# Queries and keys turned before the launch, another order of attention parts, and an earlier odd tile, in a fused attention and two-stage MoE kernel

## The chip, the cores and the metric

The kernel runs on one core of a Trainium2 chip. The metric is the device time of one execution in microseconds (us); three runs of the kernel before give the median that it is compared by. The engines are TensorE (PE, and PEld for its weight loads), VectorE (DVE), ScalarE (ACT), GpSimd (POOL), and SyncE (SP), whose queue issues nearly all transfers.

## The reference

```python
# attention: q, k, v are (4, 8, 576, 64), float32
scores = q @ k.transpose(0, 1, 3, 2) / sqrt(64)
kth = np.partition(scores, -32, axis=-1)[..., -32:-31]
scores = np.where(scores >= kth, scores, -1e9)
attn = softmax(scores);  x = (attn @ v) as (2304, 512)
# first MoE: w_a, w_b are (512, 1536), w_out (1536, 512), float64 as drawn
x = (x @ w_a) * (x @ w_b) @ w_out
# second MoE: each token goes to one of 8 experts
logits = normalise(x) @ normalise(expert_emb).T / tau
e = argmax(logits); gate = softmax(logits)[e]
out = gate * (relu(x @ w1[e]) @ w2[e])        # w1 (8, 512, 1024), w2 (8, 1024, 512)
```

Each query attends to its 32 largest scores only. Products are made nearly exact in float32 by splitting operands into a rounded high half and the low rest: three products of halves replace one.

## The kernel before

**Attention.** The work is cut into rows of 128 queries of one head against 576 keys: 144 rows. Queries come in parts, in the order of SEQ: a digit for the batch, and A (queries 0 and 1 of each four), B (2 and 3) and T (the last 64). Each part is done for four pairs of heads in turn, and a pair has two rows per head for A or B and one row for T. One loop over `step` runs the rows as a pipeline: loads ten steps ahead (AHEAD_L), turning from five (AHEAD_P), scores two ahead (AHEAD_Q), top-32 on VectorE at the step itself (`topk`: four `dve.max`, three `dve.match_replace`, then L399), softmax and the turn of the weights two to four steps later, and after a part's last row the product with the values (`mix`). `manual_schedule` fixes the order of PE, DVE, ACT and POOL as it is written out; SP's order is left to the framework.

**Turning queries and keys.** Queries and keys arrive with positions on partitions. `split_qk` makes high and low halves on POOL, `turn_qk` turns them on TensorE (`flip`, L316) into PSUM banks `tr`, and ScalarE (once VectorE) copies the result into `qT` and `kT` (L334 to L352). The first part of a batch and pair ("lead") does the keys, stores them in `kT_d`, and later parts load them from there. A score is two products: (key high, key low) with (query high, low) and with (query low, high).

**First MoE.** Tokens are done in nine groups of 256 (GROUPS), as soon as all queries of a group are there. `moe1` yields after every few matmuls (L729, L676), and `background` runs it between the attention's pieces, by a budget per step:

```python
rates.append((WORK * sum(x < w for x in opens) - spent[0]) / (w - step))
return max(min(rates, default=STEP), 0.0) + SHARE
...
share[0] = max((STEP0 if step < S0 else min(level(step), STEP)) - cost, 0.0) / max(n, 1)
```

`opens` are the steps at which groups count as open, nine after their last row (`opens.append(i + TL + 3 + RD)`), `cost` is what the step's attention costs by the planner's own figures, and `n` the number of places at which the budget is spent. The weights' halves lie in `wab_d` and are loaded again for each group. Each 128 tokens that are done are routed (`route`, L779 on): norm, logits against the expert vectors (L791), the largest, the rank within the expert, and a row written to `row_d` and its index to `ids_d`.

**Second MoE.** After the last attention row the weights of the first expert come in units of 1 MB (`unit`: load `raw`, split into `u` by ACT and DVE, L1109 and L1110), paced by the last groups of the first MoE. Tokens of the first 16 of 18 routed chunks give the first expert two full tiles (`first_expert`), which run while the last tokens are routed. Then comes its odd tile of 80 rows (`last_tile`), and then the other seven experts, each in two stages with transposed hidden values (L1179, L1353), with the next expert's rows gathered and turned (`turn_x`) in between. Only TensorE's order is written out by hand here.

## Time and profile before

| what | us |
|---|---|
| median of 3 runs (lowest to highest) | 1232.67 (1230.98 to 1233.19) |
| profiled execution, its own time | 1234.76 |
| its span, first to last instruction | 1233.0 |
| busy in the span: PE | 1133.8 (92%) |
| PEld | 982.4 (80%) |
| DVE | 916.2 (74%) |
| ACT | 822.8 (67%) |
| POOL | 728.8 (59%) |

Shares are means over stages that differ: VectorE is nearly always busy while the attention runs and little used after it. Matmul bars overlap, as matmuls are pipelined, so a step on TensorE is better priced from one start to the next than by its bar. The granted clock of TensorE is 0.97 of full over the span.

### The profile page before, as it was taken

How to read it: one execution, taken by the hardware profiler on the slowest of the kernel's cores; microseconds unless marked ns; L12 is line 12 of the kernel's file. 1: busy time of each engine (PE TensorE's matmuls, PEld its weight loads, DVE VectorE, ACT ScalarE, POOL GpSimd, SP SyncE). 2: the span in 40 equal slices, each digit the busy share in tenths (PEclk: the TensorE clock that was granted, in tenths of full speed). 3: DMA queues.
4: the chain of work that ended last, by engine and by line, in shares of the span. 5: the costliest groups of instructions: out<-in, count | busy, mean ns of one | idle time of the engine just before them, and what ended most of it. 6: DMA issues, size and time to landing. Idle time of an engine off the chain costs nothing. (4 is left out here: it accounts for less than half of the span.)

```text
span 1233.0 us, 23911 instructions
## 1 busy us (share of the span) xinstructions
PE 1133.8 (92%) x8124; PEld 982.4 (80%) x8125; DVE 916.2 (74%) x2015; ACT 822.8 (67%) x1970; POOL 728.8 (59%) x1195
## 2 busy tenths in 40 slices
PE   5767798999999998999999999999989989999996
PEld 4445566787897887898888888888878869999995
DVE  8998999999999998999999999940210225655540
ACT  5777888987878886787878877754442435554441
POOL 5565687877776876776778677665545420322211
PEclk9788899999999999999999999999999999999998
DMA  7334647676784667667666667757977245665530
GB/s 237 117 123 135 209 165 258 211 255 214 234 261 148 183 218 222 204 190 225 190 183 200 200 202 208 219 181 227 339 259 220 88 129 205 204 218 194 179 103 28
DMA packets 129200, 240.05 MB, mean 195 GB/s; under 512 B 24896, under 2 KB 74176, under 8 KB 129074
## 3 DMA queue, kind: packets, MB, share of 16 engines
q1 hardware_dynamic: 125170, 228.74, 58.6%
q0 software_dynamic: 3904, 9.75, 2.1%
q8 instruction: 65, 1.06, 0.4%
q14 instruction: 61, 0.50, 0.2%
HBM read 198.38 MB, written 40.31 MB: 194 GB/s over the span
## 5 line engine op out<-in xcount | busy, mean ns | idle before, releaser
L394 DVE MAX8 t<-y 128x8 f32<-128x576 f32 x432 | 311.7, 749 | 2.7
L409 POOL TENSOR_TENSOR z<-s,z 128x576 f32<-128x576 f32 x144 | 206.8, 1436 | 88.7 <-ACT z L406 84.1
L729 PE MATMUL ab<-xg,wab 128*128 128x256 f32 x1398 | 212.3, 290 | 3.6 <-DMA wab<-wab_d 2.0
L397 DVE MATCH_REPLACE8 y<-t,y 128x576 f32<-128x576 f32 x288 | 214.0, 743 | 0.0
L729 PEld LDWEIGHTS ab<-xg,wab 128*128 128x128 f32 x1398 | 184.2, 191 | 7.5 <-issue 2.0
L729 PE MATMUL ab<-raw,wab 128*128 128x256 f32 x1152 | 173.1, 288 | 4.0 <-ACT gab L743 3.0
L428 PE MATMUL tr<-ident,z 128*128 128x128 f32 x720 | 133.8, 285 | 45.6 <-ACT z L411 41.4
L729 PEld LDWEIGHTS ab<-raw,wab 128*128 128x128 f32 x1152 | 150.6, 189 | 6.8 <-ACT gab L743 3.6
L431 ACT ACTIVATE wt<-tr 128x384 f32<-128x384 f32 (+2 forms) x320 | 128.2, 412 | 39.9 <-PE tr L428 38.7
L374 ACT ACTIVATE s<-tr 128x288 f32<-128x288 f32 x288 | 118.0, 410 | 51.9 <-PE tr L373 41.1
L428 PEld LDWEIGHTS tr<-ident,z 128*128 128x128 f32 x720 | 88.8, 144 | 65.1 <-ACT z L411 53.8
L676 PE MATMUL x<-wo,gh 128*128 128x512 f32 x432 | 137.1, 399 | 0.0
L1163 POOL DMA_INDIRECT out_dram<-o,ids x24 | 31.4, 1307 | 170.7 <-ACT o L1162 116.5
L373 PE MATMUL tr<-kT,qT 128*128 128x288 f32 x512 | 125.5, 331 | 5.5 <-ACT s L374 4.2
L1110 DVE TENSOR_TENSOR u<-raw,u 128x1024 fp32r<-128x1024 f32 x64 | 76.2, 1222 | 60.8 <-ACT u L1109 60.8
L411 ACT ACTIVATE z<-z,bi 128x576 f32<-128x576 f32 x144 | 112.2, 779 | 0.3 <-POOL z L409 0.3
L406 ACT ACTIVATE z<-s,bi 128x576 f32<-128x576 f32 x144 | 111.3, 773 | 0.0
L663 POOL TENSOR_TENSOR gab<-gab 128x256 f32<-128x256 f32 x108 | 81.8, 757 | 49.1 <-ACT gab L743 31.2
L394 DVE MAX8 t<-s 128x8 f32<-128x576 f32 x144 | 107.1, 743 | 4.5 <-ACT s L374 4.5
L397 DVE MATCH_REPLACE8 y<-t,s 128x576 f32<-128x576 f32 x144 | 106.9, 743 | 0.0
L663 POOL TENSOR_TENSOR gl<-gab,gh 128x256 fp32r<-128x256 f32 x108 | 80.6, 747 | 44.4 <-ACT gh L663 39.8
L373 PEld LDWEIGHTS tr<-kT,qT 128*128 128x128 f32 x512 | 88.8, 205 | 15.2 <-ACT s L374 4.6
(201 smaller groups left out, 2243.5 us busy)
## 6 DMA issues: line engine op xcount, KB each, us to landing
wab<-wab_d SPq DMA_DIRECT2D x192, 512.0 KB, 4.6
raw<-in_moe_w_dram SPq DMA_DIRECT2D x28, 1024.0 KB, 5.5
wab_d<-wab SPq DMA_DIRECT2D x24, 512.0 KB, 3.9
kT<-kT_d SPq DMA_DIRECT2D x20, 576.0 KB, 5.2
vs<-in_v_dram SPq DMA_DIRECT2D x36, 256.0 KB, 3.1
kT_d<-kT SPq DMA_DIRECT2D x16, 576.0 KB, 4.6
raw<-in_moe_w_a_dram SPq DMA_DIRECT2D x12, 512.0 KB, 4.1
raw<-in_moe_w_b_dram SPq DMA_DIRECT2D x12, 512.0 KB, 4.5
```

The lines of the kernel that those rows point to most:

```text
L373: pe.matmul(p, l, r, start=(i == 0), stop=(i == len(terms) - 1))
L374: act.activation(t.s[:, cs], p, AF.Copy, scale=SCALE)
L394: dve.max(v, cur)
L397: dve.match_replace(out=rest, in_to_replace=v, in_values=cur, imm_value=LOWEST)
L406: act.activation(t.w, t.s, AF.Relu, bias=t.bi[:, 1:2], scale=-HUGE)
L409: pool.tensor_tensor(t.w, t.s, t.w, op=OP.subtract)
L411: act.activation(t.w, t.w, AF.Exp, bias=t.bi[:, 0:1], accum_out=t.o.sm[:, t.slot : t.slot + 1])
L428: pe.transpose(pt[:, i * P : (i + 1) * P], t.w[:, k0 : k0 + P], ident)
L431: act.activation(th[:, sl, w], pv[:, :, src], AF.Copy)
L663: pend.pop(0)[1]()
L676: pe.matmul(px[t], g[:, ts], wo[:, w, f], start=(f == 0 and i == 0), stop=(f == NF - 1 and i == 2))
L729: pe.matmul(ps_[i], wt[:, a, c, :], xg[x][:, c, :], start=(j == 0 and f not in begun), stop=(j == len(terms) - 1),)
```

## The change

Queries and keys are laid out by numpy before the launch, with the 64 elements of a head on the first axis and positions on the second, in the order in which the rows take them. The kernel loads each into both halves of the partitions. ScalarE rounds the high half and GpSimd subtracts the low one (VectorE for the very first part), and the turns on TensorE, their PSUM banks and evictions go. `split_qk` yields after each pair of operations, and is drawn twice a step without spending the background's budget. The two products of a score are now with the query's high half twice and with its low half twice.

The order of parts is another (SEQ): the third batch's T stands by itself, behind the fourth batch's A and T and ahead of the third's B. SHARE is smaller, and the term for turning leaves the cost. In the first MoE one forced drain of pending steps and one yield in routing are added, and yields are left out once the first expert's weights are in. A paced unit of weights is split two chunk loads later than it was. The odd tile of the first expert is gathered and turned inside `first_expert`, its hidden halves are turned between matmuls of its own two stages, and the gates that hold back the splits of later weights name both halves of a unit. The diff, cut to its core ("..." where lines are left out):

```diff
-SEQ = "0A 0B 1A 0T 1BT 2A 2BT 3AT 3B"
+SEQ = "0A 0BT 1A 1BT 2A 3AT 2T 2B 3B"
...
-SHARE = 2.1
+SHARE = 1.75
...
-FX = (0, 5)
+FX = (3, 5)
...
-    B, H, S, D = q.shape
+    B, H, D, S = q.shape
...
-    identr = cst.tile([P, P], F32R, name="identr")
-    dve.tensor_copy(identr, ident)
...
+        def both(src, dst):
+            for g in range(2):
+                sp.dma_start(dst[g * D : (g + 1) * D], src.rearrange("h d j -> d h j"))
+
         def load_q(o):
-            r = wk.tile([P, 5, D], F32, name="qr")
-            h0 = 2 * o.pr
-            for h in range(2):
-                if o.M:
-                    sp.dma_start(
-                        r[:, 2 * h : 2 * h + 2, :].rearrange("p c d -> p (c d)"),
-                        q[o.b, h0 + h, 0:512, :].rearrange("(p c) d -> p c d", c=4)[:, o.c : o.c + 2, :].rearrange(
-                            "p c d -> p (c d)"
-                        ),
-                    )
-                if o.tail:
-                    sp.dma_start(r[h * 64 : (h + 1) * 64, 4, :], q[o.b, h0 + h, 512:576, :])
+            r = wk.tile([P, 2, 320], F32, name="qr")
+            hs = slice(2 * o.pr, 2 * o.pr + 2)
+            if o.M:
+                both(q[o.b, hs, :, o.c * P : o.c * P + o.M], r[:, :, : o.M])
+            if o.tail:
+                both(q[o.b, hs, :, 512:576], r[:, :, o.M : o.N])
             return r
 
         def load_k(o, b, pr):
-            h0 = 2 * pr
-            kr = wk.tile([P, 9, D], F32, name="kr", bufs=1)
-            sp.dma_start(
-                kr[:, 0:8, :].rearrange("p (h c) d -> p h (c d)", h=2),
-                k[b, h0 : h0 + 2, 0:512, :].rearrange("h (p c) d -> p h (c d)", c=4),
-            )
-            for h in range(2):
-                sp.dma_start(kr[h * 64 : (h + 1) * 64, 8, :], k[b, h0 + h, 512:576, :])
-            o.kr = kr
-
-        def split_k(o):
-            kr = o.kr
-            ks = wk.tile([P, 9, 2, D], F32R, name="ks", bufs=1)
-            if o.n:
-                yield from split(ks[:, :, 0, :], ks[:, :, 1, :], kr)
-            else:
-                act.activation(ks[:, :, 0, :], kr, AF.Copy)
-                dve.tensor_tensor(ks[:, :, 1, :], kr, ks[:, :, 0, :].bitcast(F32), op=OP.subtract)
-            o.ks = ks
+            o.kr = wk.tile([P, 2, S], F32, name="kr", bufs=1)
+            both(k[b, 2 * pr : 2 * pr + 2], o.kr)
...
         def split_qk(o):
+
+            eng = pool if o.n else dve
             o.qT = wk.tile([P, 2, 512], F32R, name="qT")
             o.kT = wk.tile([P, 2, S], F32R, name="kT", bufs=2)
             o.wt = [None, None]
             o.sm = wk.tile([P, 8], F32, name="sm", bufs=3)
             o.rc = wk.tile([P, 8], F32, name="rc", bufs=3)
+            todo = []
+            if o.lead:
+                for h in range(2):
+                    todo.append((o.kT[:, h], o.kT[D:, h], o.kr[:, h], o.kr[D:, h], h))
+            else:
+                sp.dma_start(o.kT.bitcast(F32).rearrange("p h j -> p (h j)"), kT_d[o.b * NP + o.pr])
+            if o.M:
+                hi, lo = (o.qT[:, a].rearrange("p (h j) -> p h j", h=2) for a in range(2))
+                todo.append((hi, lo, o.qr[:, :, : o.M], o.qr[:, :, : o.M], 0))
             if o.tail:
                 o.qm = qms.pop(0)
                 qms.append(o.qm)
                 for h in range(2):
+                    hi, lo = (o.qm[:, a, h, h * 64 : (h + 1) * 64] for a in range(2))
+                    r = o.qr[:, h, o.M : o.N]
+                    todo.append((hi, lo, r, r, 0))
+            due = None
+            for hi, lo, r, x, last in todo + [(None,) * 5]:
+                if due:
+                    lo_, x_, hi_, last_ = due
+                    eng.tensor_tensor(lo_, x_, hi_.bitcast(F32), op=OP.subtract)
+                    if last_:
+                        sp.dma_start(kT_d[o.b * NP + o.pr], o.kT.bitcast(F32).rearrange("p h j -> p (h j)"))
+                if r is None:
+                    return
+                act.activation(hi, r, AF.Copy)
+                due = lo, x, (lo if lo.shape[0] != hi.shape[0] else hi), last
+                yield
 
...
-            if o.lead:
-                yield from split_k(o)
-            qs = wk.tile([P, 5, 3, D], F32R, name="qs", bufs=1)
-            js = slice(0 if o.M else 4, 5 if o.tail else 4)
-            yield from split(qs[:, js, 0, :], qs[:, js, 1, :], qr[:, js])
-            pool.tensor_scalar(qs[:, js, 2, :], qr[:, js], 1.0, 1.0, op0=OP.mult, op1=OP.mult)
-            o.qs = qs
...
-            def flip(pt, c, x):
-                pe.transpose(pt[:, c * P : (c + 1) * P], x.rearrange("p a d -> p (a d)"), identr)
...
-            for a in range(2 if o.M else 0):
-                pt = ps.tile([P, 512], F32R, name="tr", bufs=NTR)
-                for c in range(4):
-                    flip(pt, c, qs[:, c, a : a + 2, :])
-                if a or o.n:
-                    act.activation(o.qT[:, a, :], pt.bitcast(F32), AF.Copy)
-                else:
-                    dve.tensor_copy(o.qT[:, a, :], pt.bitcast(F32))
-                yield 0.22
...
+                while pend and pend[0][0] <= f - 2:
+                    tick()
...
+            if now[0] >= NRW and not ended:
+                yield 0.0
...
             act.activation(lg, pl[:, :NE], AF.Copy)
-            yield 0.0
+            if not ended:
+                yield 0.0
...
             if flips and (flips[0].n < 2 or parts[flips[0].n - 2].left == 0):
-                while flips[0].qs is None:
-                    piece()
-                if not run(flips[0].flip):
-                    flips.pop(0)
+                with tc.high_priority(offset=FG):
+                    if next(flips[0].flip, flips) is flips:
+                        flips.pop(0)
...
-            if flips:
-                cost, n = cost + 0.44, n + 2
...
+                if slot_ == 2:
+                    flip_next()
             if 0 <= step + AHEAD_Q < NRW:
                 live[step + AHEAD_Q].o.left -= 1
-            for _ in range(2):
-                flip_next()
...
+                    if i and c == 2:
+                        split_unit(i - 1)
             else:
                 sp.dma_start(raw, src)
+                split_unit(i)
+
+        def split_unit(i):
+            raw = raws.pop(i)
             u = w2p.tile([P, 2, 4, 512], F32R, name="u", bufs=UB)
             if gate[0] is not None:
-                act.activation(u[:, 0, 0, 0:1], gate[0], AF.Copy)
+                act.activation(u[:, 0, 0:4:2, 0:1], gate[0], AF.Copy)
...
+        def split(pt, x, xT, m):
+            for c in range(KC):
+                pe.transpose(pt[:, c * P : c * P + m], x[:m, c * P : (c + 1) * P], ident[:m, :m])
+            pv = pt.rearrange("p (c j) -> p c j", c=KC)[:, :, :m]
+            hi, lo = xT
+            act.activation(hi, pv, AF.Copy)
+            dve.tensor_tensor(lo, pv, hi.bitcast(F32), op=OP.subtract)
...
+                    if (t, f) == (1, 5):
+                        reached.append(f)
...
+        split_unit(UB - 1)
+        ended.append(True)
...
+        spare = wx.tile([P, 2, KC, m0], F32R, name="yT", bufs=1)
+        x0 = wx.tile([P, RW], F32, name="xg", bufs=2 * NT3)
+        x0T = [spare[:, i] for i in range(2)]
+        pick(x0, ids[0][:m0, NT3 - 1, 0:1])
+        while not reached:
+            next(early0)
+        split(bank("tr"), x0, x0T, m0)
+        for _ in early0:
+            pass
...
-            t, m = NT3 - 1, m0
-            xs = [None] * t + [wx.tile([P, RW], F32, name="xg", bufs=2 * NT3)]
-            xT = [wk.tile([P, KC, cap], F32R, name=f"xT{i}")[:, :, : caps[0]] for i in range(2)]
-            hT = [wk.tile([P, NF2, cap], F32R, name=f"hT{i}", bufs=1)[:, :, :m] for i in range(2)]
-            pick(xs[t], ids[0][:m, t, 0:1])
+            hT = [wk.tile([P, NF2, cap], F32R, name=f"hT{i}", bufs=1)[:, :, :m0] for i in range(2)]
             nx = gather(NE - 1)
-            turn_x((xs, xT), t)
-            hs = []
+            hs = [result(), x0[:, :DM]]
+
+            def turn_h(half):
+                split(bank("tr"), hs[half], [y[:, half * 4 : half * 4 + 4] for y in hT], m0)
+
             for half in range(2):
                 u = units[half]
                 p = bank("h")
                 n = 0
                 for a, b in TERMS:
                     for c in range(KC):
-                        pe.matmul(p[:m], xT[b][:, c, t * P :], u[:, a, c, :], start=(n == 0), stop=(n == 11))
+                        pe.matmul(p[:m0], x0T[b][:, c, :], u[:, a, c, :], start=(n == 0), stop=(n == 11))
                         n += 1
-                hs.append(result())
-                act.activation(hs[-1][:m], p[:m], AF.Relu)
+                        if half and n == 7:
+                            turn_h(0)
+                act.activation(hs[half][:m0], p[:m0], AF.Relu)
             turn_x(nx, 0, NE - 1)
-            for half, h in enumerate(hs):
-                pt = bank("tr")
-                for j in range(4):
-                    pe.transpose(pt[:, j * P : j * P + m], h[:m, j * P : (j + 1) * P], ident[:m, :m])
-                pv = pt.rearrange("p (j k) -> p j k", j=4)[:, :, :m]
-                hi, lo = (y[:, half * 4 : half * 4 + 4] for y in hT)
-                act.activation(hi, pv, AF.Copy)
-                dve.tensor_tensor(lo, pv, hi.bitcast(F32), op=OP.subtract)
-            gate[0] = hT[0][:, 4, 0:1]
-            upto(2 + UB)
             p = bank("y")
             for f in range(NF2):
                 stage2(0, f, p, hT[0][:, f], hT[1][:, f])
+                if f == 1:
+                    turn_h(1)
                 if f in FX:
                     turn_x(nx, 1 + FX.index(f), NE - 1)
-            put(p, xs[t], ids[0][:m, t, 1:2], m, result())
+                if f == FX[0]:
+                    gate[0] = hT[0][:, 4:6, 0:1]
+                    upto(2 + UB)
+            put(p, x0, ids[0][:m0, NT3 - 1, 1:2], m0, result())
             return nx
...
-                if f % 4 == 0:
+                if f == 0 or (f == 4 and e > 1):
...
-                            gate[0] = hT[0][:, NF2 - 1, 0:1] if f == 0 else None
+                            gate[0] = hT[0][:, NF2 - 2 :, 0:1] if f == 0 else None
...
+def turned(a):
+
+    import numpy as _np
+
+    b, h, _, d = a.shape
+    rows = a[:, :, :512].reshape(b, h, 128, 4, d).transpose(0, 1, 4, 3, 2).reshape(b, h, d, 512)
```

## Rows read from the trace of the kernel before

**Rows 1.** Windows, all engines: length, busy us and instructions per engine, TensorE clock, DMA.
```profile
250.00:455.00 205.00, 200.13 (x1607) 173.97 (x1606) 203.38 (x475) 167.93 (x448) 157.44 (x281) 1.00 0.68 212
...
669.00:778.00 109.00, 105.13 (x794) 88.98 (x793) 102.51 (x237) 86.22 (x221) 78.03 (x144) 0.98 0.67 200
778.00:826.00 48.00, 46.44 (x357) 42.07 (x357) 35.43 (x88) 31.40 (x79) 32.17 (x62) 1.00 0.66 205
```
**Rows 2.** The same windows, line L399 alone, which runs once for each row.
```profile
250.00:455.00 205.00, 5.40 (x40) 1.00 0.68 212
455.00:669.00 214.00, 5.43 (x40) 0.99 0.68 208
669.00:778.00 109.00, 2.71 (x20) 0.98 0.67 200
778.00:826.00 48.00, 1.10 (x8) 1.00 0.66 205
```
**Rows 3.** Line L316 (PE: ns min/median/max), then its windows: PE, PEld.
```profile
L316 PE MATMUL tr<-identr,qs x288: 219/247/369, 6.7 to 770.7; 128*128 128x128 f32 x144
...
L316 PE MATMUL tr<-identr,ks x144: 220/248/367, 5.5 to 686.1; 128*128 128x128 f32 x144
...
455.00:669.00 214.00, 14.29 (x118) 12.73 (x118) 0.99 0.68 208
669.00:778.00 109.00, 6.03 (x51) 5.36 (x51) 0.98 0.67 200
```
**Rows 4.** Timeline of PE around four turns: start us, length us, what.
```profile
405.94 0.46 PE L316 MATMUL tr<-identr,ks 128*128 128x128 f32 x4
406.23 0.70 PE L729 MATMUL ab<-xg,wab 128*128 128x256 f32 x4
```
**Rows 5.** Timeline of the start.
```profile
3.95 0.68 ACT L264 ACTIVATE ks<-kr 128x576 fp32r<-128x576 f32 x1 [1.69 <-DMA kr<-in_k_dram]
4.66 0.76 DVE L265 TENSOR_TENSOR ks<-kr,ks 128x576 fp32r<-128x576 f32 x1 [0.86 <-ACT ks L264]
...
8.29 2.37 PE L373 MATMUL tr<-kT,qT 128*128 128x288 f32 x8 [0.37 <-DVE qT L352]
```
**Rows 6.** Groups by form: count, busy us, mean ns, idle before.
```profile
L350 ACT ACTIVATE qT<-tr 128x512 fp32r<-128x512 f32 x63 | 37.4, 608 | 2.7 <-PE tr L316 2.5
...
L229 POOL TENSOR_TENSOR ks<-kr,ks 128x576 fp32r<-128x576 f32 x15 | 21.5, 1434 | 0.4
```
**Rows 7.** Timeline of PE, the sixth group's beginning, its end, and the seventh's beginning.
```profile
675.22 0.63 PE L729 MATMUL ab<-raw,wab 128*128 128x256 f32 x4
...
765.97 0.55 PE L428 MATMUL tr<-ident,z 128*128 128x128 f32 x3 [0.70 <-ACT z L411]
...
770.41 0.53 PE L316 MATMUL tr<-identr,qs 128*128 128x128 f32 x4 [1.02 <-POOL qs L302]
771.88 0.90 PE L428 MATMUL tr<-ident,z 128*128 128x128 f32 x3 [0.94 <-ACT z L411]
...
777.52 0.75 PE L729 MATMUL ab<-xg,wab 128*128 128x256 f32 x4
```
**Rows 8.** Timeline of PE near the first MoE's end.
```profile
894.27 1.68 PE L729 MATMUL ab<-raw,wab 128*128 128x256 f32 x12
...
921.19 1.15 PE L791 MATMUL ab<-enT,x1T 128*128 128x8 f32 x8 [3.03 <-ACT x1T L787]
922.19 2.91 PE L729 MATMUL ab<-xg,wab 128*128 128x256 f32 x12
```
**Rows 9.** Timeline of PE, the first expert's odd tile and the second expert.
```profile
1000.82 5.74 PE L1297 MATMUL h<-u,xT 128*80 128x512 f32 x24 [1.02 <-ACT xT L1158]
...
1010.44 0.53 PE L1305 MATMUL tr<-ident,o 80*128 80x80 f32 x4 [3.16 <-DVE xT L1159]
1010.84 1.57 PE L1191 MATMUL y<-u,hT 128*80 128x512 f32 x3
...
1034.78 1.36 PE L1353 MATMUL y<-hT,u 128*128 128x264 f32 x9 [1.49 <-DVE hT L1184]
```

More of the change, by code (lines that the diff above doesn't have):

```diff
@@ L345, in turn_qk @@
-            for a in range(2 if o.M else 0):
-                pt = ps.tile([P, 512], F32R, name="tr", bufs=NTR)
-                for c in range(4):
-                    flip(pt, c, qs[:, c, a : a + 2, :])
-                if a or o.n:
-                    act.activation(o.qT[:, a, :], pt.bitcast(F32), AF.Copy)
-                else:
-                    dve.tensor_copy(o.qT[:, a, :], pt.bitcast(F32))
-                yield 0.22
+                    hi, lo = (o.qm[:, a, h, h * 64 : (h + 1) * 64] for a in range(2))
@@ L806, in route @@
             dve.tensor_scalar(st[:, 2:3], m8[:, 0:1], st[:, 1:2], -1.0, op0=OP.mult, op1=OP.mult)
-            yield 0.0
+            if not ended:
+                yield 0.0
             ex = mk.tile([P, NE], F32, name="ex")
@@ L1004, in fused_kernel @@
                 en_turn(mp, e_sb)
-            for o in coming[:1]:
-                if step >= o.first - AHEAD_P or (step >= o.first - AHEAD_P - 2 and not flips):
-                    pieces.append(split_qk(o))
-                    coming.pop(0)
-                    while step < EAGER and pieces:
-                        piece()
+            while step < EAGER and pieces:
+                piece()
             while 0 <= step + AHEAD_Q < NRW and live[step + AHEAD_Q].o in flips:
@@ L1091, in unit @@
             e = slice(0, 1) if n == 0 else bass.ds(expert[NE - n], 1)
-            raw = w2p.tile([P, 4, 512], F32, name="raw", bufs=2)
+            raws[i] = raw = w2p.tile([P, 4, 512], F32, name="raw", bufs=2)
             if part < 2:
@@ L1111, in unit @@
             units[i] = u
-        units = {}
+        units, raws = {}, {}
         expert = [0] * NE
@@ L1152, in turn_x @@
             m = rows_of(r)[t]
-            pt = bank("tr")
-            for c in range(KC):
-                pe.transpose(pt[:, c * P : c * P + m], xs[t][:m, c * P : (c + 1) * P], ident[:m, :m])
-            pv = pt.rearrange("p (c j) -> p c j", c=KC)[:, :, :m]
-            hi, lo = (y[:, :, t * P : t * P + m] for y in xT)
-            act.activation(hi, pv, AF.Copy)
-            dve.tensor_tensor(lo, pv, hi.bitcast(F32), op=OP.subtract)
+            split(bank("tr"), xs[t], [y[:, :, t * P : t * P + m] for y in xT], m)
         def put(p, xg, ids, m, o):
@@ L1240, in fused_kernel @@
                 next(early0, None)
-        for _ in early0:
-            pass
-        mo.close()
-        if "xh" in dbg:
-            sp.dma_start(dbg["xh"][:, :, : batches * S], xh_d[:, :, : batches * S])
-            sp.dma_start(dbg["xl"][:, :, : batches * S], xl_d[:, :, : batches * S])
-        if "row" in dbg:
-            nr = sum(GROUPS[done - 1])
-            sp.dma_start(dbg["row"][:nr], row_d[1 : nr + 1])
-            sp.dma_start(dbg["ids"], ids_d)
-        if batches < 4:
-            return
-        wk = ph.enter_context(tc.tile_pool(name="wk2", bufs=2))
         m0 = rows_of(0)[-1]
@@ L1271, in fused_kernel @@
             )
+        spare = wx.tile([P, 2, KC, m0], F32R, name="yT", bufs=1)
[7 more added lines that the diff above has]
+            pass
+        mo.close()
+        if "xh" in dbg:
+            sp.dma_start(dbg["xh"][:, :, : batches * S], xh_d[:, :, : batches * S])
+            sp.dma_start(dbg["xl"][:, :, : batches * S], xl_d[:, :, : batches * S])
+        if "row" in dbg:
+            nr = sum(GROUPS[done - 1])
+            sp.dma_start(dbg["row"][:nr], row_d[1 : nr + 1])
+            sp.dma_start(dbg["ids"], ids_d)
+        if batches < 4:
+            return
+        wk = ph.enter_context(tc.tile_pool(name="wk2", bufs=2))
         banks.append(ph.enter_context(tc.tile_pool(name="ps3", bufs=1, space=PSUM)))
```

38 lines of the change are left out of this document (6 added, 32 removed).

## The prediction

> **What bounds the kernel now.** I read the windows first, all engines, over the attention from its row 36 on. (A "row" is one pass of the loop: 128 queries of one head, four MAX8 and three MATCH_REPLACE8 on VectorE.) From 250 to 455 us VectorE is busy 203.4 of 205 us and TensorE 200.1: both are full [rows 1]. To know which sets the pace I counted rows by L399, which runs once a row: 40 rows in 205 us, 5.125 us each, with VectorE idle 1.6 us in all, so VectorE sets it there; then 40 in 214 us, 20 in 109, and 8 in 48, which is 6.0 us a row [rows 2]. In that last stretch VectorE is busy only 35.4 of 48 us while TensorE has 46.4 [rows 1]: there TensorE sets the pace. The four counts and 36 rows before them are all 144, so after about 826 us no row is left, and TensorE carries the rest alone. There are two regimes, then, and TensorE work that is taken out is worth something only where TensorE is last, or where the freed time is filled with MoE work that is otherwise done after the attention. After that I read TensorE's timeline at the seam between two token groups, at the longest wait of the first MoE's end, and in the last part; they stand with the steps that they price.
>
> **The change, part by part.**
>
> *The turns go.* The code has 9 turns for each of 16 first parts, 8 for each of 32 parts with 256 queries and 2 for each of 16 tails: 144 + 256 + 32 = 432, and the trace has 288 + 144 [rows 3]. Four of them end 0.29 us after they begin (405.94 to 406.23), though their bars last 0.46 [rows 4], so one costs 0.0725 us and all 31 us. 51 of them lie in 669 to 778 us, 118 in 455 to 669 [rows 3], and the others before, where VectorE sets the pace or TensorE has idle time anyway.
>
> *What replaces them.* ScalarE loses the evictions (63 of the queries' are 37.4 us; half as many of the keys' and small ones come on top) and gets one 128x576 copy per head of keys (32 at L264's 0.68 us, 21.8 us [rows 5]), one 128x512 copy per part (32 at L350's 0.608 us, 19.5 us) and 32 small copies: about even [rows 6]. GpSimd loses the rounding passes and the 15 key subtractions over 128x576, 21.5 us, and gets 30 subtractions of as many columns on 64 partitions; at the same 1.434 us that is 43 us [rows 6], 21.5 more, against the passes that go. I take this at nothing, because GpSimd is idle 47.6 of 205 us from 250 to 455 [rows 1]; what it costs if a subtraction comes late is the second rival. The loads of queries and keys move twice the bytes (a copy each for the upper and the lower partitions), in 16 fewer issues (two per key load where three were). They are issued ten rows ahead, some 51 us at 5.125 us a row, and the reload of keys from kT_d stays at 20 issues; SP's queue has nothing new to wait for. Nothing again.
>
> *The start.* The first score matmul runs at 8.29 us. Now three copies on ScalarE and three subtractions on VectorE come before it, where copy, subtraction, turn and eviction were. Copies of 0.68 us from the landing at 3.95, and subtractions of 0.76 behind the first of them (L264, L265 [rows 5]), end at about 7.0, so that the score matmul can go at 7.1. I take 1.2 us; bounds 0 and 1.5.
>
> *Rows 36 to 116.* 250 to 455 us has nothing to give: VectorE is full. In the next 40 rows, 214 us against 40 x 5.125 = 205, there are 9 us that VectorE loses to late scores and sums. 118 turns fall here, 8.6 us of TensorE. I take 5 of the 9; bounds 0 and 9, since part of it may come from the seams between groups, which stay.
>
> *The new order and SHARE.* The planner counts a group as open nine rows after its last query row. By the old order that is at rows 24, 40, 56, 80, 96, 116, 136, 136, 152; by the new one at 24, 44, 60, 80, 96, 116, 120, 136, 152. Its rate is the smallest of (46.3 x groups open before w, less what is spent) / (w - row), plus SHARE, at most STEP = 5.4. Old: from row 24 on 46.3 x 6 / 112 = 2.48 a row up to row 136, and there 2 x 46.3 for 12 rows, over the cap. New: about 2.5 up to row 116, and there (370.4 - 231.5) / 36 = 3.9, plus 1.75 = 5.6: the cap holds from row 116 on. The attention's own cost in the planner's units is 0.54 + 0.48 + about 0.7, 1.7 a row, so 3.7 a row goes to the MoE for 32 rows, where it was 2.5 for the first 20 of them. A row at the cap takes 6.0 us [rows 2], so the attention ends later: rows 116 to 144 take 28 x 6.0 = 168 us instead of 157. That costs nothing in itself, because TensorE is then full all the way and the work it does comes off the end. From row 116 to the end of the first MoE I therefore count TensorE alone. The 51 turns go (51 x 0.0725 = 3.7 us). The sixth group (675 to 767 us) no longer waits for its successor, which is open at row 120: the idle 0.70, 1.02 and 0.94 us there go, with some 1.5 us of a half clock behind them (three transposes took 0.90 us, where they had taken 0.55), 4.2 us [rows 7]. Together 7.9; bounds 0 and 7.9.
>
> *The end of the first MoE.* Group routing now yields once more before its logits, and ScalarE no longer stands at the raw weights' landing, as a unit is split two chunks later. The 3.03 us that TensorE waits for x1T at 921 us, and the 12 matmuls behind it that take 2.91 us where 1.68 is usual [rows 8], make 4.4 us with a few slow matmuls more. I take all; bounds 0 and 4.4.
>
> *The last part.* TensorE waits 1.02 us for the odd tile's xT, 3.16 for DVE xT, and 1.49 for DVE hT [rows 9]. The tile is now fetched and turned inside the expert before, the second ReLU writes to a buffer of its own, and the weights' splits are gated behind both halves. With a half clock after the 3.16 (three matmuls take 1.57 us) that is 6.7 us; I take 6.0, as the fetch may come late at its new place; bounds 2 and 6.7.
>
> **Sum.** 1234.76 - 1.2 - 5 - 7.9 - 4.4 - 6.0 = 1210.3 us for the profiled execution, whose span is 1233.0. The median of the runs is 1232.67, 2.1 lower, so I forecast 1208. With all bounds at their ends it is 1203 to 1231.
>
> **A rule against this sum.** By TensorE's weight-load time, 174.0 of 205 us from 250 to 455, a seventh of it would be free where its matmul bars show it full [rows 1]. The Trainium skill (Perfetto Trace Analysis, section Identifying the Most-Contended Engine) says that the bars are the poorer measure of headroom and the weight loads the better one. What it would make of the time is the third rival, at 1184 instead of 1208.
>
> **The rivals.**
>
> *The freed time is not filled.* VectorE sets the pace up to row 116, and the planner's pace is fixed when the program is written, so that it can't react. If groups become ready later than it counts (stores and reloads of xh and xl), rows 116 to 136 run as before, and what is left is the start, the wait for x1T and the last part: 1232.7 - 11.6 = 1221. For it: those 20 rows take 109 us as it is, with both engines near full [rows 1, 2]. Against: the seams at 675 and 777.5 us come within two rows of the planner's 116 (669 us) and 136 (778 us) [rows 2, 7].
>
> *Slower.* The low halves are now the last step before the scores, on GpSimd, whose queue also holds the mask subtraction that waits for ScalarE. If one subtraction of 1.434 us [rows 6] stands in the way of each of the 32 full parts, VectorE loses 32 x 1.43 = 46 us: 1254. It decides from 24.5 / 32 = 0.77 us a part. For it: GpSimd is three quarters busy [rows 1]. Against: lists of at most six pieces are drawn two to a row from five rows ahead, and scores start two rows ahead.
>
> *TensorE has room in the attention.* If 15% of its time, 0.77 us a row, can still be filled, the 32 rows at the cap take that much more work without growing: 32 x 0.77 = 24.6 us, 1184. Against it: at the cap a row takes 6.0 us while VectorE is idle a quarter of it [rows 1, 2].
>
> **How the numbers follow.** Forecast 0.69 (own range 1199 to 1219); not filled 0.14; slower 0.09; room 0.05; no change at all, since gains and losses cancel, 0.03. Less than 0.2% (2.5 us) can't be told from no change here. Faster 0.69 + 0.14 + 0.05 = 0.88, same 0.03, slower 0.09. The range 1193 to 1228 leaves out the slower case, the case of room, no change, and some 3 in 100 of the rest.
>
> **What would show it.** No L316; score matmuls that wait for GpSimd no more than the turns did; rows 36 to 76 still at about 5.1 us; the rows after row 116 at about 6 us, with TensorE without idle; no pause between the sixth and the seventh group; the last row later than 826 us, and the last part beginning some 18 us earlier; no wait over 1 us in its first 20 us. The prediction is wrong if rows before 116 take over 5.3 us, if score matmuls wait for GpSimd, or if weights (wab) come late in the stretch at the cap.

## The result, and the profile after

The changed kernel takes 1223.87 us in the median of four runs (1214.99 to 1226.78), the kernel before 1232.93 us beside it: a ratio of 0.9898, 95% interval 0.9868 to 0.9927 (the two medians alone divide to 0.9927; the ratio is what is compared below). The forecast was 1208 us, range 1193 to 1228: the sign and the range hold, the medians' gain of 9.1 us is less than half of the 24.5 that were summed. The profiled execution took 1223.5 us, its span 1221.6 us.

I cut both spans at the same marks: the first pass of the row marker (L399 before, L354 now), its rows 36 and 116, and the eviction that begins the last block's routing, with which the first MoE ends. In us:

| stretch | before | after | difference | forecast |
|---|---|---|---|---|
| start to row 0 | 18.3 | 21.4 | +3.1 | -1.2 |
| rows 0 to 36 | 232.1 | 223.9 | -8.2 | 0 |
| rows 36 to 116 | 418.9 | 431.6 | +12.7 | -5 |
| row 116 to the end of the first MoE | 306.1 | 291.4 | -14.7 | -12.3 (7.9 and 4.4) |
| last part | 257.6 | 253.3 | -4.3 | -6.0 |
| sum | 1233.0 | 1221.6 | -11.4 | -24.5 |

**The attention.** The windows of the changed kernel, all engines: length, then busy us and instructions of PE, PEld, DVE, ACT and POOL, TensorE's clock, DMA share and GB/s.
```profile
245.30:676.90 431.60, 401.95 (x2987) 341.46 (x2987) 409.29 (x951) 336.37 (x870) 333.60 (x541) 0.98 0.75 226
676.90:829.20 152.30, 150.66 (x1157) 134.17 (x1158) 124.29 (x296) 109.15 (x273) 107.69 (x196) 1.00 0.74 232
...
309.40:391.10 81.70, 77.99 (x587) 67.71 (x586) 81.32 (x187) 64.99 (x169) 60.92 (x105) 1.00 0.76 218
391.10:610.70 219.60, 204.89 (x1514) 174.66 (x1514) 204.86 (x479) 171.50 (x440) 175.04 (x275) 0.98 0.72 217
```
The first line is rows 36 to 116. VectorE has 409.3 us of work for 80 rows, 5.116 each, which is its floor; 22.3 us are idle. The third line is rows 48 to 64, and they stand at the floor (5.11 us a row). The fourth is rows 64 to 104, which take 5.49; before, these rows stood so:
```profile
393.50:606.20 212.70, 205.84 (x1584) 177.89 (x1583) 204.66 (x479) 168.89 (x439) 161.04 (x271) 0.99 0.66 201
```
The second, rows 116 to 140, is the stretch at the cap: TensorE is idle 1.6 of 152.3 us, and a row takes 6.35.

What VectorE and TensorE wait for in rows 36 to 116 (total us, times, longest), a view for each engine:
```profile
DVE rc L394 <- POOL rc L392: 15.2, 12, 2.4
DVE st L760 <- POOL st L754: 3.6, 1, 3.6
DVE t L349 <- ACT s L329: 1.6, 1, 1.6
...
PE tr L383 <- ACT z L366: 22.0, 24, 4.1
```
Before, the first stood at 6.1 us in 5 waits and the last at 6.3 us in 6. The timeline shows one of the waits for the sum, in row 46, GpSimd and then VectorE:
```profile
295.93 0.74 POOL L619 TENSOR_TENSOR gl<-gab,gh 128x256 fp32r<-128x256 f32 x1 [2.24 <-ACT lg L757]
297.42 0.74 POOL L619 TENSOR_TENSOR gab<-gab 128x256 f32<-128x256 f32 x1 [0.76 <-ACT gab L701]
...
298.32 1.44 POOL L364 TENSOR_TENSOR z<-s,z 128x576 f32<-128x576 f32 x1
299.83 0.24 POOL L392 TENSOR_SCALAR rc<-sm 128x4 f32<-128x4 f32 x1
...
297.48 0.19 DVE L767 TENSOR_SCALAR st<-m,st 128x1 f32<-128x1 f32 x1
300.11 0.18 DVE L394 RECIPROCAL rc<-rc 128x4 f32<-128x4 f32 x1 [2.43 <-POOL rc L392]
```
The sums are complete at 298.1, when the exponential has ended; the addition of 1e-9 stands behind the next row's mask subtraction on GpSimd, and VectorE, in order, behind the addition. No low half stands in GpSimd's queue here: it had itself stood 2.24 and 0.76 us for ScalarE. The longest wait, VectorE's 3.6 us for the router's `st`, is in row 73, which took 8.7 us; GpSimd, and then TensorE:
```profile
430.50 1.12 POOL L799 DMA_INDIRECT ids_d<-tk,ds  x1 [0.29 <-POOL ds L798]
...
436.15 1.42 POOL L301 TENSOR_TENSOR kT<-kr,kT 64x576 fp32r<-64x576 f32 x1 [3.33 <-DMA ids_d<-tk,ds]
...
441.99 0.90 PE L383 MATMUL tr<-ident,z 128*128 128x128 f32 x3 [4.12 <-ACT z L366]
```
GpSimd stood still for 3.33 us ahead of a key subtraction until the routing's index write, issued at 430.50, had landed; behind it in the queue stood a mask subtraction, a low half of queries and then `st`. TensorE, which had stood 4.12 us, was at its lower clock, 1.2 GHz (granted 0.50), from 439.4 to 446.2 us, and its three transposes took 0.90 us where 0.55 is usual.

GpSimd's new work, line L301: its form for keys (ns min/median/max), then its windows in the two stretches (VectorE, GpSimd).
```profile
L301 POOL TENSOR_TENSOR kT<-kr,kT x30: 1401/1424/1488, 17.2 to 579.4; 64x576 fp32r<-64x576 f32 x30
```
```profile
309.40:391.10 81.70, 0.00 (x0) 5.86 (x9) 1.00 0.76 218
391.10:610.70 219.60, 0.00 (x0) 36.39 (x34) 0.98 0.72 217
```
The low halves take GpSimd 5.9 us in the rows at the floor and 36.4 us in the slow stretch, whose 34 instructions hold 16 key subtractions of 1.42 us; before, GpSimd had 161.0 us of work in these rows, now 175.0. A subtraction over 64 partitions costs what one over 128 did [rows 6].

**The start.** ScalarE, VectorE and TensorE, each by its timeline:
```profile
6.16 1.25 ACT L306 ACTIVATE kT<-kr 128x576 fp32r<-128x576 f32 x2 [3.90 <-DMA kr<-in_k_dram]
...
16.34 0.68 ACT L306 ACTIVATE kT<-kr 128x576 fp32r<-128x576 f32 x1 [5.24 <-DMA kr<-in_k_dram]
...
17.97 0.76 DVE L349 MAX8 t<-s 128x8 f32<-128x576 f32 x1 [2.28 <-ACT s L329]
...
9.08 3.49 PE L328 MATMUL tr<-kT,qT 128*128 128x288 f32 x13 [0.49 <-DVE qT L301]
```
The first copy runs at 6.16 us where it ran at 3.95 [rows 5]: the keys, twice the bytes, land 2.2 us later (6.1 us in the median from issue to landing in the first 27 us, before 3.9). The second pair's keys land at 16.3 us, with VectorE waiting behind.

**The seam, the end of the first MoE, the last part**, in TensorE's timeline:
```profile
749.71 0.62 PE L632 MATMUL x<-wo,gh 128*128 128x512 f32 x2
750.17 0.64 PE L685 MATMUL ab<-xg,wab 128*128 128x256 f32 x4
...
915.48 2.16 PE L685 MATMUL ab<-xg,wab 128*128 128x256 f32 x16
917.52 1.06 PE L751 MATMUL ab<-enT,x1T 128*128 128x8 f32 x8
918.43 0.72 PE L685 MATMUL ab<-xg,wab 128*128 128x256 f32 x4
...
992.60 4.54 PE L1270 MATMUL h<-u,yT 128*80 128x512 f32 x19
996.98 0.44 PE L1112 MATMUL tr<-ident,o 80*128 80x80 f32 x4
997.21 1.35 PE L1270 MATMUL h<-u,yT 128*80 128x512 f32 x5
...
1007.04 0.50 PE L1141 MATMUL h<-xT,u 128*128 128x264 f32 x2 [0.56 <-DVE u L1070]
...
1017.84 3.19 PE L1141 MATMUL h<-xT,u 128*128 128x264 f32 x24 [0.88 <-DVE hT L1146]
```
The seventh group follows the sixth without a pause, at 750 where it was 777.5 us [rows 7]. The router's matmuls no longer wait for x1T, and nothing runs slow behind them [rows 8]. The waits of 1.02, 3.16 and 1.49 us of [rows 9] are gone; small ones, the two longest shown, take their place.

### The profile page after: what moved, and what is told of

Same layout as the page of the kernel before. It is cut to its first block, busy times and chain, and to the rows that moved or that the text cites. A ratio compares the mean times of both kernels' runs of the same rounds, so it can differ in the third digit from the quotient of the medians.

```text
span 1221.6 us, 22925 instructions
## 1 busy us (share of the span) xinstructions
PE 1098.5 (90%) x7692; PEld 940.3 (77%) x7693; DVE 916.3 (75%) x2014; ACT 810.7 (66%) x1923; POOL 732.0 (60%) x1150
## 3 DMA queue, kind: packets, MB, share of 16 engines
q8 instruction: 62, 1.02, 0.3%
## 5 line engine op out<-in xcount | busy, mean ns | idle before, releaser
L685 PE MATMUL ab<-xg,wab 128*128 128x256 f32 x1398 | 207.3, 289 | 1.8 <-DMA wab<-wab_d 1.8
L685 PEld LDWEIGHTS ab<-xg,wab 128*128 128x128 f32 x1398 | 183.3, 191 | 4.8 <-DMA wab<-wab_d 2.4
L685 PE MATMUL ab<-raw,wab 128*128 128x256 f32 x1152 | 170.4, 290 | 3.6 <-ACT gab L701 3.5
L685 PEld LDWEIGHTS ab<-raw,wab 128*128 128x128 f32 x1152 | 150.7, 192 | 6.9 <-ACT gab L701 4.5
```

Of the source, the lines that this page charges most:

```text
L685: pe.matmul(ps_[i], wt[:, a, c, :], xg[x][:, c, :], start=(j == 0 and f not in begun), stop=(j == len(terms) - 1),)
```

## The experiments

Each was timed beside the kernel before on its own chip. The stretches (us) are those of the table above, from the profiled executions, which differ from the medians by up to some 8 us (those of e2 and e3 were the slowest of their runs).

| run | ratio, 95% interval | row 0 | 0-36 | 36-116 | to end of first MoE | last |
|---|---|---|---|---|---|---|
| changed kernel | 0.9898 (0.9868-0.9927) | 21.4 | 223.9 | 431.6 | 291.4 | 253.3 |
| e1 key low halves on VectorE | 1.0006 (0.9988-1.0024) | 27.1 | 227.7 | 434.6 | 286.3 | 254.0 |
| e2 old order | 1.0095 (1.0060-1.0131) | 21.4 | 231.4 | 438.9 | 310.5 | 253.0 |
| e3 three key tiles | 0.9868 (0.9838-0.9899) | 24.8 | 225.6 | 430.5 | 291.2 | 255.2 |
| e4 before + last part | 0.9914 (0.9883-0.9944) | 18.7 | 231.4 | 419.7 | 302.8 | 253.6 |
| e5 sums on VectorE | 0.9865 (0.9830-0.9900) | 21.2 | 225.7 | 425.6 | 285.8 | 252.1 |
| e6 e5 with SHARE 2.1 | 1.0043 (1.0018-1.0068) | 21.3 | 231.6 | 439.2 | 290.6 | 252.0 |
| e7 e5 with the old order | 1.0136 (1.0102-1.0170) | 21.3 | 233.5 | 432.2 | 304.2 | 252.2 |
| e8 e4 with sums on VectorE | 0.9946 (0.9926-0.9967) | 18.4 | 230.7 | 419.7 | 300.2 | 252.3 |
| e9 no negation | 0.9810 (0.9780-0.9840) | 21.7 | 220.6 | 428.8 | 289.9 | 252.4 |
| e10 no addition | 0.9885 (0.9845-0.9924) | 21.3 | 224.6 | 428.6 | 290.4 | 256.1 |
| e11 three key tiles, e9, e10 | 0.9846 (0.9803-0.9888) | 26.2 | 225.1 | 422.1 | 288.7 | 252.5 |
| e12 e4 with e9, e10 | 0.9897 (0.9867-0.9927) | 18.2 | 230.4 | 418.2 | 298.7 | 252.2 |

**e1, the keys' low halves on VectorE.**
```
-    eng.tensor_tensor(lo_, x_, hi_.bitcast(F32), op=OP.subtract)
+    (dve if lo_.shape[0] < P else eng).tensor_tensor(lo_, x_, hi_.bitcast(F32), op=OP.subtract)
```


> The changed kernel with its 28 later key subtractions on VectorE in place of GpSimd (the first two are on VectorE already); nothing is left out. Theory 1, GpSimd is the engine that is late in rows 36 to 116: 20 of the 28 lie there or just before, 1.42 us each, so GpSimd loses about 28 us of work there and VectorE gains under 20 us against some 75 us of idle time in that stretch; the VectorE waits on the sum of GpSimd (15.2 us in 12 waits in 250 to 676) go back to about the 6 us of before, and rows 36 to 116 from 431.6 to 419 to 423 us; median 1212 to 1217, ratio to before 0.983 to 0.987. Theory 2, the order of the parts makes the stretch long: rows 36 to 116 stay within 3 us of 431.6 and the ratio within 0.988 to 0.993. Theory 3, VectorE was short: rows 36 to 116 get longer by the added VectorE work, up to 15 us, ratio up to 1.0.

Rows 36 to 116, VectorE's only waits, and the window:
```profile
DVE kT L301 <- ACT kT L306: 1.0, 2, 0.5
```
```profile
254.70:689.40 434.70, 403.32 (x3024) 342.69 (x3022) 431.09 (x971) 338.21 (x874) 311.30 (x528) 0.99 0.74 224
```
The waits of 20.4 us fall to 1.0: without the key subtractions on GpSimd VectorE doesn't wait for it at all. But VectorE is the engine that sets the pace there, and has 431.1 us of work in 434.7. Theory 3 holds for the time, theory 1 for the waits. (At the start VectorE now stands 10.9 us for copies of keys, and row 0 comes 5.7 us later.) It doesn't show that the stretch would fall to 410 us if the subtractions cost nothing, since a slower VectorE also gives the others more time in each row.

**e2, the old order.**
```
-SEQ = "0A 0BT 1A 1BT 2A 3AT 2T 2B 3B"
+SEQ = "0A 0B 1A 0T 1BT 2A 2BT 3AT 3B"
```


> The changed kernel with the parts in the order of before; the rest as in the changed kernel. Theory 2, the order (two batches' leads next to each other, the first group opened four rows later) costs rows 36 to 116: they go from 431.6 to at most 421 us, row times above 5.8 us vanish, and the median falls by 8 to 12 us, ratio about 0.980 to 0.984, unless the end of the attention gives some of it back because its tail by itself stands late again. Theory 1, GpSimd late whatever the order: the same sum of row times, its late rows only spread over other places; ratio 0.988 to 0.994. Opposite: the new order is what shortened rows 0 to 36 or row 116 to the end of the first expert layer, and the old one gives that back: ratio 0.995 or more.

The opposite case came: slower than the changed kernel by 2%, and worse in each stretch from row 0 to the end of the first MoE (+7.5, +7.3, +19.1 us). In rows 36 to 116, VectorE's and TensorE's longest waits:
```profile
DVE rc L394 <- POOL rc L392: 16.8, 10, 3.1
DVE t L349 <- ACT s L329: 7.8, 8, 3.5
...
PE tr L383 <- ACT z L366: 37.8, 27, 6.2
```
Theory 2 falls: the new order doesn't cost rows 36 to 116, it helps them. GpSimd's lateness is there in either order; in the old one rows 56 to 64 take 46.2 us, where 40.7 is the floor, with no key subtraction in them. The new order by itself, with turns on TensorE, wasn't tried.

**e3, three key tiles of one head.**
```
-    o.kr = wk.tile([P, 2, S], F32, name="kr", bufs=1)
-    both(k[b, 2 * pr : 2 * pr + 2], o.kr)
+    o.kr = []
+    for h in range(2):
+        o.kr.append(wk.tile([P, 1, S], F32, name="kr", bufs=3))
+        both(k[b, 2 * pr + h : 2 * pr + h + 1], o.kr[h])
...
```


> The changed kernel with the key tile cut into one for each head and three of them in place of the one tile for both heads, so that the next pair's first head is loaded while the pair before is still being split; four loads for each pair in place of two. If late key data cost time: the row marker 0 comes 2 to 3 us earlier (21.4 to about 18.5), the 3.3 us stand of GpSimd before the key subtraction at 432.8 goes, its 5.9 us of such waits between 250 and 676 fall below 2, and the median falls by 3 to 8 us, ratio 0.983 to 0.988. If they were covered behind the first rows' other work and GpSimd's slack: ratio within 0.003 of 0.990 and only the start moves.

The first score matmul and VectorE's first weight unpacking:
```profile
7.77 3.90 PE L330 MATMUL tr<-kT,qT 128*128 128x288 f32 x14 [7.77 <-ACT qT L308]
...
14.38 0.43 DVE L503 TENSOR_SCALAR w64t<-raw 128x512 int32<-128x512 int32 x1 [5.94 <-DMA raw<-in_moe_w_a_dram]
```
The scores run from 7.77 us on, where all but one ran from 9.08, but the next keys are now fetched ahead of the weights, for which VectorE, in order, waits 5.9 us; row 0 comes 3.4 us later. The other stretches are as in the changed kernel within 2 us, and the ratio can't be told from its. GpSimd's stand ahead of that key subtraction, which the expectation took for late key data, is still there, 4.0 us long: it ends at 442.25 us, and the last landing of the index write is at 442.13.

**e4, the last part alone**: the kernel before with FX, the split of the weights in two steps, the odd tile's early fetch, the placed turns and the router's extra yield.

> The kernel before with only the edits to its last part (expert stage: the first expert's gather and turn set ahead of the end of the first layers, turns of its hidden rows placed between the matmuls, second weight's split in two steps, corrections at other blocks). Forecast of the document: minus 4.4 at the end of the first layers and minus 6.0 after, together minus 10.4 (2 to 11.1). What the two traces show: the last part took 4.3 us less in the changed kernel, and the wait at the end of the first layers (3.03 us and the half clock behind it) was gone. If the gains of the parts add up: minus 5 to minus 9 us, ratio 0.9927 to 0.996. If the wait at the end of the first layers went for another reason (the pacing there): minus 3 to minus 5 us, ratio 0.996 to 0.9975.

8.7 us below the median of before, at the upper end of what adds up; the profile has -3.3 to the end of the first MoE and -4.0 after. The changed kernel's whole gain is hardly more: its interval overlaps this one's over most of its width.

**e5 to e8, the sums on VectorE.** The edit of e5:
```
     if add:
-        pool.tensor_scalar(o.rc[:, sl], o.sm[:, sl], 1e-9, None, op0=OP.add)
         return
+    dve.tensor_scalar(o.rc[:, sl], o.sm[:, sl], 1e-9, None, op0=OP.add)
     dve.reciprocal(o.rc[:, sl], o.rc[:, sl])
```


> The changed kernel with the small addition to the softmax sums done on VectorE, next to the reciprocal that reads it, in place of GpSimd one row earlier; nothing is left out. Theory 1, GpSimd's queue: in rows 36 to 116 VectorE's reciprocal stood 15.2 us behind that addition, which takes 0.08 us and stood in GpSimd's queue behind the next row's mask subtraction (1.43 us) and low halves, while the last exponential that it needs had ended 0.3 to 3 us before it; counted wait by wait from the exponentials' ends, 1.3 of the 15.2 us are left. So rows 36 to 116 go from 431.6 to 417 to 421 us; if this comes through to the end, the median falls by 10 to 14 us, ratio 0.978 to 0.982. Rival: the wait only moves, to late scores or masks, or TensorE's backlog is what sets the end: rows 36 to 116 at 425 us or more and ratio 0.986 to 0.992.

Rows 36 to 116 are 6 us shorter, half of what theory 1 said: the waits for the sum fall from 15.2 to 0.9 us, but VectorE's busy time in the stretch rises by 9.8 (419.1, before 409.3). The additions take, once begun, min/median/max ns
```profile
L393 DVE TENSOR_SCALAR rc<-sm x36: 134/170/2465, 49.6 to 864.1; 128x4 f32<-128x4 f32 x20, 128x5 f32<-128x5 f32 x12, 128x1 f32<-128x1 f32 x4
```
and the longest of them stands thus beside GpSimd:
```profile
559.26 2.46 DVE L393 TENSOR_SCALAR rc<-sm 128x5 f32<-128x5 f32 x1
...
558.60 1.13 POOL L799 DMA_INDIRECT ids_d<-tk,ds  x1 [0.29 <-POOL ds L798]
559.76 0.26 POOL L363 TENSOR_SCALAR bi<-t 128x1 f32<-128x1 f32 x1
559.96 1.45 POOL L364 TENSOR_TENSOR z<-s,z 128x576 f32<-128x576 f32 x1
561.35 0.33 POOL L301 TENSOR_TENSOR qm<-qr,qm 128x64 fp32r<-128x64 f32 x1
```
It ends at 561.72, when four GpSimd instructions without a gap between them have ended (561.68). So part of the wait changed its name. The ratio's interval overlaps the changed kernel's.

> As the one with the sums on VectorE, and SHARE back at 2.1 from 1.75, so that more expert work goes into each row where the cap doesn't hold. If TensorE runs dry in rows 36 to 116 since its turns are gone and the pace was lowered (PE stands 22.4 us in 28 waits for the exponentials there, 6.5 in 8 before), more work fills that: PE's idle time there falls, rows stay at 5.1 to 5.2 us, and the time falls by up to 8 us more, ratio 0.972 to 0.979. If the pace hardly binds or groups aren't ready: within 0.002 of the run with the sums alone. If VectorE waits for scores behind the added work: rows 36 to 116 get longer by 5 us or more and the ratio rises by 0.002 or more.

```
-SHARE = 1.75
+SHARE = 2.1
```
Slower, by 1.8% against e5. TensorE's idle time in rows 36 to 116 rises from 24.8 to 41.7 us and rows take longer. VectorE's waits are now for scores and exponentials (9.1 and 8.6 us). But these rows hold no more of the first MoE's work: 1176 matmuls of L685, in e5 1220, and 31 more lie before row 36. So the run shows that the larger share is slower, not that it fills the rows more; why it is slower stays open.

> The changed kernel with the old order of parts and the sums on VectorE. With the old order alone rows 36 to 116 took 438.9 us, with 16.8 us of VectorE's waits for the sum and 8.0 for scores. Theory 1: 10.5 of the 16.8 go, rows 36 to 116 at 427 to 430, ratio from 1.0095 to 0.999 to 1.003. If the old order loses its time elsewhere (TensorE stands 42 us in those rows), ratio 1.006 or more; the order's own worth is then the difference to the changed kernel with the sums on VectorE.

1.0136: no better than with the old order alone. Rows 36 to 116 gain 6.7 us and the ratio nothing.

> The kernel before with the new last part and with the sums on VectorE (queries and keys still turned on TensorE, old order). Its waits for the sum in rows 36 to 116 were 6.6 us, of which 0.4 would be left by the exponentials' ends. Theory 1: 5 to 7 us less than with the last part alone, ratio 0.9914 to 0.986 to 0.988. If this wait is hidden: ratio 0.990 to 0.993. If this comes out level with or below the changed kernel with the sums on VectorE, the new way of queries and keys and the new order are together worth nothing here.

0.9946, no better than e4, with rows 36 to 116 at the same 419.7 us: the wait for the sum was no cost there. With the old way of queries and keys theory 1 has nothing to say.

**e9 and e10, each half of the chain.** e9 leaves out the negation `pool.tensor_scalar(t.bi[:, 0:1], t.top, -1.0, ...)` and the exponential's bias; e10 the addition, so that the reciprocal reads `o.sm`.

> The changed kernel without the negation of the row's maximum on GpSimd (0.22 us a row): the exponential leaves out the subtraction of the maximum, which drops out of the quotient. GpSimd loses 80 x 0.22 = 17.6 us in rows 36 to 116 and nothing else changes; the mask subtraction can start 0.2 us earlier in each row. Theory 1a, GpSimd's load: VectorE's 15.2 us of waits for the sum there fall below 11, rows 36 to 116 from 431.6 to 422 to 428 us, ratio 0.982 to 0.987. Theory 1b, only the place in the queue matters (the addition still stands behind the next row's mask subtraction): waits 13 us or more, rows 36 to 116 at 429 or more, ratio 0.987 to 0.992.

> The changed kernel without the addition of 1e-9 to the softmax sums: VectorE's reciprocal reads the sums directly. Against the run with that addition on VectorE, VectorE also loses the 10.9 us that 21 additions took in rows 36 to 116 (0.16 us when GpSimd stood still, up to 2.47 us when it worked without a pause). Theory 1b: rows 36 to 116 at 414 to 420 us, 12 to 17 below the changed kernel, which is the forecast step made good; median 11 to 16 us below it, ratio 0.977 to 0.982. Rival, the time of the additions was time in which VectorE would have stood for GpSimd in any case (the reciprocal or the next row's instruction takes the stand over): rows 36 to 116 at 424 or more and the ratio within 0.003 of 0.9865.

e9 is 0.981, the lowest of all, its interval below the changed kernel's. Two links of the chain are shorter, against the expectation, which said that nothing else changes: GpSimd's by 0.22 us a row, and ScalarE's exponential, which no longer reads a bias, by 0.09 (changed kernel, then e9; ns min/median/max):
```profile
L366 ACT ACTIVATE z<-z,bi x144: 758/772/842, 27.4 to 872.0; 128x576 f32<-128x576 f32 x144
...
L365 ACT ACTIVATE z<-z x144: 665/682/759, 28.0 to 863.6; 128x576 f32<-128x576 f32 x144
```
Which of the two counts wasn't told apart. Yet rows 36 to 116 give only 2.8 us and the sum still waits 13.9 us there; the rest lies in rows 0 to 36 (-3.3) and after row 116 (-2.5). e10 moves the time by less than the interval. VectorE's waits there in e10:
```profile
DVE rc L393 <- ACT z L366: 5.6, 6, 2.9
DVE t L349 <- ACT s L329: 5.1, 12, 1.0
DVE st L759 <- POOL st L753: 5.0, 2, 4.7
```
16 us in place of 20: the wait for the sum was where the lateness showed, not its cause. Taken away, it comes back as waits for exponentials, scores and the router. The rival of e10 held.

> The changed kernel with no addition, no negation (both left out of the computation) and three key tiles. If the three add up: rows 36 to 116 at 411 to 416 us, close to VectorE's floor of 80 x 5.12 = 410; the start not above 21.4; median 1203 to 1210, ratio 0.975 to 0.981. If VectorE's floor is reached with the addition gone alone, no more than 0.002 below that run.

> The kernel before with the new last part, without the addition and without the negation: queries and keys are still turned on TensorE, and the order is the old one. It tells what the new way of queries and keys and the new order are worth when GpSimd's queue is relieved in both. Forecast by the terms of the document without the edits to queries, keys and order: rows 36 to 116 go from 419.7 to 411 to 414; ratio 0.985 to 0.989. If it is at or below the changed kernel with the same two left out, the new front and order together bring nothing; by the document's terms (turns and seams after row 116, 7.9 us; start) it should stay 6 to 10 us above it.

e11 leaves out both and has three key tiles: rows 36 to 116 at 422.1 us, 6 above the range expected, and the late row 0 of e3 once more. It is no better than e9. e12, with turns on TensorE and the old order, stands at 0.9897, 418.2 us in rows 36 to 116, 4 above the range expected. Its median is 4.4 us above e11's, where 6 to 10 were expected; that, 0.005 in the ratios, is what the new way of queries and keys and the new order may be worth with the chain relieved (e11 has e3's tiles and late start as well); the intervals overlap. The two omissions take 1.5 us off rows 36 to 116 in the old front (turns on TensorE, old order; e4 to e12) and 9.5 in the new one (changed kernel to e11, of which the key tiles alone gave 1.1 in e3).

## Why the prediction was right, and where it was wrong

*The turns go: right in number, worth nothing before row 116.* No L316 is left. By L316's windows 147 of the 432 turns lay in rows 0 to 36 and 234 in rows 36 to 116, 27.6 us at 0.0725 (my "118" was its second half alone). TensorE's idle time up to row 116 rose from 69.4 to 101.0 us (length less busy time, both windows), by 31.6: so all that was freed there became idle time. The first MoE's matmuls of L729, now L685, hardly grew in rows 36 to 116 (1176 to 1208); the plan puts no more of them there. The prediction said so of its first 40 rows, and hoped for 5 us in the next.

*What replaces them, "I take this at nothing": the step that failed.* The average hid it. GpSimd is busy 77% of rows 36 to 116, but it works in order, and the mask subtractions, on which exponential, turn, scores and the reciprocal hang, stand behind whatever it has. TensorE stood 22 us for exponentials and VectorE 20.4 us, its three waits above, for what follows. Of the 12.7 us by which these rows grew, 6.9 are rows 64 to 104 (212.7 to 219.6), with 16 key subtractions and 14 us more work for GpSimd; 2.7 are rows 44 to 48, nearly all of it row 46, where no key subtraction stands in the queue; 1.0 rows 104 to 112; and 2.1 rows 112 to 116, which already run at the cap. The rest stayed: rows 48 to 64, without key subtractions, at 81.7 us, but also rows 36 to 44, with four of them and half the first MoE's matmuls (53, before 107), at 40.7. By the prediction's own sign, rows before 116 over 5.3 us, it is wrong here: these 80 take 5.395. Its other two signs, scores that wait for GpSimd and late wab at the cap, didn't come (0.7 and 0.2 us of TensorE's waits).

The rival called slower named the mechanism, but put it ahead of the scores and at 46 us; it was 12.7 at most, in the chain of the mask. e1 shows that taking the key subtractions off GpSimd ends VectorE's waits, though VectorE is slower there too; e11 and e12 that shortening the chain on GpSimd and ScalarE is worth some 8 us in these rows with the new front and 1.5 with the old; e10 that the addition behind which VectorE stood isn't the cause. That this chain is the late link is shown, then; that the key subtractions make it late is only argued. Of the ten waits for the sum over 0.5 us, none has a key subtraction among GpSimd's instructions of the 4 us before it, and the wait of 3.6 us for `st` came after GpSimd's own stand for a landing. How much of the 12.7 us they cost stays open: no run had them gone without work added elsewhere.

*The start: wrong by 4.3 us.* "Nothing again" for twice the bytes: the loads' landing is the path there, 2.2 us later for the first pair and more for the second. In e3, with a head's keys by themselves, ScalarE's first copy runs at 4.36 us.

*Rows 0 to 36, not in the sum: -8.2 us.* Nearly all of it is rows 24 to 36 (87.3 to 80.7). It takes the new order and the smaller SHARE together: with the old order (e2) these 36 rows take 231.4 us, and with SHARE at 2.1 (e6) 231.6. Why wasn't tried; VectorE's waits there for weight data and sums fell from 9.8 to 2.1 us.

*The new order and the cap: right.* From row 116 on -14.7 us; in e4, without them, -3.3, so some 11 us belong to the turns, the seam and the order, where 7.9 were summed. TensorE has almost no idle time at the cap (1.6 us in 24 rows), group seven follows at once, and the attention ends later (row 143 at 848 us), as worked out. The rival "not filled" didn't come there: L729's matmuls, now L685's, in rows 116 to 143 rose from 469 to 637. Nor did "room": the rows at the cap grew with the work, from 6.0 to 6.35 us. The last part begins 7.1 us earlier (968.3, before 975.4), where the prediction had some 18.

*The end of the first MoE and the last part: right, but 7.3 of the 10.4 us came.* e4 alone has -3.3 and -4.0 for 4.4 and 6.0; small waits took the place of the large ones.

Together: two terms missed (17.7 and 4.3 us), one found that I hadn't summed (8.2), the others within 2.4. That the time lies in the range is in part luck: without the 8.2 us, which no term held, it would have been some 1232, and the forecast's own narrower range, 1199 to 1219, was missed. Measured by runs, the last part's edits account for most of the whole gain; the new way of queries and keys without the new order costs some 2% (e2 against e4, SHARE differing too), and the new order gives that back.

## What to carry to other kernels

Work taken off an engine is worth something only in the stretch where that engine comes last; count what is left to fill it with. Work moved to an engine with a quarter of its time free need not be free if that engine is a link in a chain of in-order queues: look at what stands behind it there, part by part, and at what the engine itself waits for, and not at the share of busy time. And the wait with the most time in a table need not be the cause: when it was removed, three others took its place, while a small cut further up the chain (e9, 0.31 us a row on GpSimd and ScalarE, which beats both kernels at 0.981, leaving out the maximum's subtraction) was worth more.

## What the runs showed of the hardware

A VectorE addition over 128x5 elements took 0.16 us when GpSimd stood still and up to 2.46 us beside GpSimd instructions without a gap, and ended as the fourth of them did (e5); the key subtraction on VectorE took 0.75 to 2.02 us (e1), while MAX8 beside the same GpSimd work stayed at 0.74. The Trainium skill (SBUF — State Buffer, section SBUF: two separate sides) says that VectorE and GpSimd have one pair of ports in common, which one instruction locks for its whole length, and that only some kinds of VectorE instructions want it; these durations agree. That an instruction so small stood through four others, and not through one, I hadn't expected, and no run here explains it.

An exponential over 128x576 elements on ScalarE took 0.772 us in the median with a bias read for each partition and 0.682 without (changed kernel, e9).
